# Moving small vector work to GpSimd and keeping joined weight words in PSUM, in a fused attention and two-layer MoE kernel

## The chip, the cores and the metric

The kernel runs on one core of a Trainium2 chip. The metric is the device time of one execution in microseconds (us). A core has five engines that the text names as the profile does: PE (TensorE, matrix products; PEld are its weight loads), DVE (VectorE), ACT (ScalarE), POOL (GpSimd) and SP (SyncE, which here issues nearly all DMAs). Each engine works through its own list of instructions in order and waits on semaphores for the others. PE writes its results to PSUM, a memory of eight banks of 2 KB per partition; the other data lie in SBUF. A row of scores of 768 float32 numbers takes 3 KB, and so two banks.

## What is computed

```
q_bucket, k_bucket = sign bits of q @ proj and k @ proj (6 bits), read as one number
scores = q @ k.T / 8, kept where the buckets are equal, else -1e9
attn   = softmax(scores);  x = attn @ v          # 2 batches, 8 heads, 768 x 768, head size 64
h = x @ w_in;  g = elu(h);  x2 = g @ w_out       # 1536 tokens, 512 -> 2048 -> 512
h = x2 @ w_in2;  g = s * relu(h)**2 + b;  out = g @ w_out2
```

The inputs are float64 in memory. The kernel builds float32 words from their two 32-bit halves with integer operations, and then splits each number into two float16 parts, a high one and the rest, so that three float16 products give nearly a float32 one.

## The kernel before, in words

One **unit** is one head of one block of 128 query rows: 2 x 6 x 8 = 96 units, counted u = 0 to 95 (`unit`). Of each unit, `u_s` makes the scores (four matmuls, L345), `u_soft` clamps them and takes the row's minimum on DVE (L355), makes the exponential's bias `mx` from it (L356, one number per row, DVE), and lets ACT take the exponential (L357). `u_split` transposes the result: for the first 16 units on PE (L366, L369), afterwards by splitting it into float16 parts (ACT L376, POOL L379) and a transposing DMA (L381). `u_av` multiplies by v (L393, L399). After eight units `u_norm` scales the block, casts it to float16 (L420, DVE), and takes the rest on POOL (L421).

Before the units of a batch can run, `p_split`, `p_bits` and `p_buck` prepare each pair of heads hp: they scale and split q and k (L247, L252), copy rows (L264), transpose by DMA (L270, L271, L279), copy halves of the transposed tiles (L282, L313), and add the bucket code (L307, L310, L320, L324).

Weights are made by `w_stream`, one chunk of 128 x 512 numbers at a step: a DMA loads it (L167), three DVE operations join the halves into a word (L187, L188, L190), ACT rounds it to the high part (L181), DVE takes the rest (L194). The first two joins write the PSUM tile `wx`; the third writes the SBUF tile `wa`, and both L181 and L194 read `wa`.

The order has two stages around the change. In the **first stage** the units run alone with the 16 chunks of `w_in`, until two blocks are done; PSUM then holds one score tile (`ps_s0`), two tiles for transposes and bucket codes (`ps_p0`), one bank for `wx` and one for the sums over v. In the **second stage** the products of the first layer (`moe1`: `up` gives L515 h, `down` gives L515 x2p) run, and between their steps a credit counter calls `w1_step` (16 chunks of `w_out`) and `att_step` (half a unit). PSUM then has two banks for products, two score tiles (`ps_s`, NS = 2) that also serve the bucket codes, and one bank for `wx`. Before unit 40's half step, `att_step` runs `w1_step` until all weights are made. From then on there are more buffers for the attention. The second layer (`moe2`) follows when the attention is over. A scheduler places the instructions of each engine in order of program priority and of its own estimate of when they can start; within one engine that order is then fixed.

`Ring.take(kind, ...)` gives out the pools of a kind in turn, with one counter for each kind.

Of the kernel before, what the change touches and what calls it, by code (L numbers as in the profile page):

```python
# [7 lines left out]
F32 = mybir.dt.float32  # L8
# [3 lines left out]
ACTF = mybir.ActivationFunctionType  # L12
ALU = mybir.AluOpType
PSUM = bass.MemoryType.PSUM
# [4 lines left out]
PT = 4  # L19
EX = dict(p=1, ph=1, pt=1, raw=2)  # L20
NP = 3
LOAD = [(-4, -4), (-3, -2)]
SPLIT0 = [(-4, -4), (-3, -3), (-2, -2), (0, 1)]
ENG0 = ['dve', 'act', 'act', 'act']
BITS0 = [-2, -1, 1, 3]
BUCK0 = [1, 0, 1, 1]
# [37 lines left out]
def model_kernel(tc, q, k, v, proj, w_in, w_out, w_in2, w_out2, s2, b2, sel, pop, eye, out):  # L64
# [24 lines left out]
    with ExitStack() as base:  # L89
# [18 lines left out]
        ps_w = pool(base, "ps_w", 1, space=PSUM)  # L108
        ps_s = [pool(st0, "ps_s0", S0, space=PSUM)]
        ps_p = [pool(st0, "ps_p0", P0, space=PSUM) if P0 else ps_s[0]]  # L110
        ps_m = []

        class Ring:
# [7 lines left out]
            def take(self, kind, shape, dt, name):  # L121
                pools = self.sets[kind]
                self.n[kind] += 1
                tag = "m" if kind == "w" else kind
                return pools[self.n[kind] % len(pools)].tile(shape, dt, tag=tag, name=name)
# [11 lines left out]
        ring = Ring()  # L137
        ring.use(p=[unp] * NP + [p0] * 2, ph=[un3] * NPH + [h0] * H0N, pt=[ptp] * PT + [t0_] * T0N, raw=[raw0])

        def w_raw(st):  # L140
            return pool(st, "wraw", WRAW, side="right")
# [90 lines left out]
        def p_load(b, hp, nm):  # L232
# [10 lines left out]
            raws[b, hp, nm] = t  # L243

        def scaled(eng, out, in_, sg):
            if eng == "act":
                nc.scalar.activation(out=out, in_=in_, func=ACTF.Copy, scale=sg)  # L247
            else:
                nc.vector.tensor_scalar(out, in_, sg, None, op0=ALU.mult)
# [7 lines left out]
        def p_split(b, hp, nm, eng):  # L257
# [3 lines left out]
            if nm == "k":  # L261
                hi = s_[:, :, :, 0, :]
                scaled(eng, hi, t, SQ)
                nc.vector.tensor_copy(out=s_[:, :, :, 1, :], in_=hi)  # L264
                l_ = ring.take("ph", [128, C, 2, D], F16, "srcl")
                for j in range(2):
                    rest(l_[:, :, j, :], t[:, j], SQ, hi[:, j])
                o1 = per.tile([128, 2, C, 128], F16, tag=f"k1{hp}", name=f"k1{hp}")
                o2 = per.tile([128, 2, C, 128], F16, tag=f"k2{hp}", name=f"k2{hp}")
                nc.sync.dma_start_transpose(out=full(o1), in_=s_.rearrange("p h c x d -> p (h c x d)"))  # L270
                nc.sync.dma_start_transpose(out=o2[:, 0], in_=l_.rearrange("p c x d -> p (c x d)"))  # L271
                k1[b, hp], k2[b, hp] = o1, o2
                return
# [7 lines left out]
            for j in range(2):  # L281
                nc.vector.tensor_copy(out=o2[D * j:D * j + D, j], in_=o1[D * j:D * j + D, j])  # L282
            q1[b, hp], q2[b, hp] = o1, o2
# [12 lines left out]
        def p_bits(b, hp):  # L296
            p = ps_p[0].tile([128, S], F32, tag="s", name="pbit")
            flat = lambda z: z.rearrange("p c t -> p (c t)")
# [13 lines left out]
            o = k2[b, hp]  # L312
            nc.vector.tensor_copy(out=o[D:2 * D, 1], in_=o[D:2 * D, 0])  # L313

        def p_buck(b, hp):
            t = bits.pop((b, hp))
            for x, (o, sc) in enumerate(((k2[b, hp], BK), (q2[b, hp], -BQ))):
                p = ps_p[0].tile([128, S], F32, tag="s", name="pone")
                for a0, a1 in halves:
# [19 lines left out]
        def u_s(u):  # L339
            b, c, h, hp, j = unit(u)  # L340
            p = ps_s[0].tile([128, S], F32, tag="s", name="s")
            for x, (w, m) in enumerate(((q1, k1), (q2, k2))):
# [6 lines left out]
        def u_soft(u):  # L349
# [5 lines left out]
            nc.vector.tensor_scalar(f, sps.pop(u), CLAMP, None, op0=ALU.min, op1=ALU.min, accum_out=mx)  # L355
            nc.vector.tensor_scalar(mx, mx, sm / (SQ * SQ), 10.0 * LN2, op0=ALU.mult, op1=ALU.add)  # L356
            nc.scalar.activation(out=f, in_=f, func=ACTF.Exp, scale=-sm / (SQ * SQ), bias=mx,  # L357
# [3 lines left out]
        def u_split(u, eng):  # L361
            f = pf.pop(u)
            if u < FC * H:
                p = ps_p[0].tile([128, S], F32, tag="s", name="pT")
                for cc in range(C):
# [44 lines left out]
        def u_norm(b, c):  # L410
# [8 lines left out]
            fl = xf.rearrange("p h d -> p (h d)")  # L419
            nc.vector.tensor_copy(out=xh[:, 0, :], in_=fl)  # L420
            nc.gpsimd.tensor_tensor(out=xh[:, 1, :], in0=fl, in1=xh[:, 0, :], op=ALU.subtract)  # L421
# [274 lines left out]
        if True:  # L696
# [3 lines left out]
            for hp, nm in ((0, "k"), (0, "q"), (1, "k"), (1, "q")):  # L700
# [4 lines left out]
            wst = pool(wdst, "wst", WST, side="right")  # L705
            wdec = w_raw(wdst), lambda: (wst.tile([128, 512], F32, tag="wa", name="wa"),
                                         ring.take("w", [128, 512], F32, "wx"))
            ws1 = w_stream(w_in_chunks(wi, w_in), *wdec)
# [9 lines left out]
            ring.use(m=ps_m[:])  # L718
            ps_s[0] = ps_p[0] = pool(ast, "ps_s", NS, space=PSUM)
            wop = pool(w1st, "wop", 1)  # L720
# [14 lines left out]
            def w1_step():  # L735
                if live["w1"] and next(ws1, 0) == 0:
                    live["w1"] = False
                    wdst.close()
                    ps_m.append(ps_w)
                    ring.use(m=ps_m[:])  # L740
                    ex = {k_: right(exst, f"ex_{k_}", n_) for k_, n_ in EX.items() if n_}
# [97 lines left out]
```

## Time and profile before

| | us |
|---|---|
| runs | 733.87, 735.33, 736.55 (median 735.33) |
| profiled execution | 734.32 |
| its span, first to last instruction | 732.5 |
| PE busy | 673.8 (92%) |
| DVE busy | 469.8 (64%) |
| ACT busy | 381.8 (52%) |
| POOL busy | 263.8 (36%) |

Busy time is the union of an engine's instructions. A busy PE need not be a PE at its peak, since matmuls are pipelined and their ends are modelled. The shares are means over stages with different limits, so the rows further down are taken by stage.

### The profile page before, as it was taken

How to read it: one execution, taken by the hardware profiler on the slowest of the kernel's cores; microseconds unless marked ns; L12 is line 12 of the kernel's file. 1: busy time of each engine (PE TensorE's matmuls, PEld its weight loads, DVE VectorE, ACT ScalarE, POOL GpSimd, SP SyncE). 2: the span in 40 equal slices, each digit the busy share in tenths (PEclk: the TensorE clock that was granted, in tenths of full speed). 3: DMA queues.
4: the chain of work that ended last, by engine and by line, in shares of the span. 5: the costliest groups of instructions: out<-in, count | busy, mean ns of one | idle time of the engine just before them, and what ended most of it. 6: DMA issues, size and time to landing. Idle time of an engine off the chain costs nothing.

```text
span 732.5 us, 14396 instructions
## 1 busy us (share of the span) xinstructions
PE 673.8 (92%) x5808; PEld 465.1 (63%) x5808; DVE 469.8 (64%) x874; ACT 381.8 (52%) x648; POOL 263.8 (36%) x199
## 2 busy tenths in 40 slices
PE   2779787988888999999999999999999999999998
PEld 0368666776676777888888888854444444444446
DVE  5789989989877477746744765258898989100000
ACT  2897777955698788656754413135555553010000
POOL 0000355843354388756754403124444441000000
PEclk9999979999999999999999999999999999999999
DMA  9985599999798789666658440002222214010000
GB/s 221 257 219 139 142 229 222 191 224 241 159 204 185 114 145 169 126 126 110 124 108 124 131 145 1 2 29 87 87 86 87 87 58 144 1 72 15 30 29 30
DMA packets 206594, 89.67 MB, mean 122 GB/s; under 512 B 171840, under 2 KB 203072, under 8 KB 206528
## 3 DMA queue, kind: packets, MB, share of 16 engines
q1 hardware_dynamic: 205936, 88.63, 54.8%
q8 instruction: 45, 0.74, 0.4%
q14 instruction: 21, 0.17, 0.1%
q10 hardware_dynamic: 592, 0.14, 0.1%
HBM read 43.13 MB, written 3.15 MB: 63 GB/s over the span
## 4 chain that ended last, share of the span: by engine, by line
PE 60%; DMA 13%; DVE 12%; ACT 7%; issue 6%; POOL 2%; SPq 0%; DVEq 0%; ACTq 0%; POOLq 0%
PE h L515 24%; PE y L515 17%; PE x2p L515 10%; DMA pt<-ph 8%; PE s L345 3%; PE xacc L399 3%; DVE p L355 3%; DVE e L530 2%; ACT p L357 2%; DMA q<-src 2%; POOL ph L379 1%; DVE wx L188 1%; ACT gh L535 1%; DMA k<-src 1%; ACT ph L376 1%
## 5 line engine op out<-in xcount | busy, mean ns | idle before, releaser
L379 POOL TENSOR_TENSOR ph<-p,ph 128x768 f16<-128x768 f32 x80 | 134.1, 1680 | 121.6 <-ACT ph L376 89.3
L515 PE MATMUL h<-x,wih 128*128 128x256 f16 x768 | 131.3, 275 | 0.1
L357 ACT ACTIVATE p<-p,mx 128x768 f32<-128x768 f32 x96 | 89.2, 929 | 55.1 <-DVE mx L356 53.6
L355 DVE TENSOR_SCALAR_CACHE_REDUCE p<-s 128x768 f32<-128x768 f32 x96 | 91.0, 951 | 36.9 <-PE s L345 34.5
L515 PE MATMUL x2p<-gh,wol 128*128 128x256 f16 x384 | 105.2, 275 | 1.4 <-DVE wol L194 1.4
L515 PE MATMUL x2p<-gh,woh 128*128 128x256 f16 x384 | 105.0, 275 | 1.6 <-ACT woh L181 0.9
L515 PE MATMUL x2p<-gl,woh 128*128 128x256 f16 x384 | 105.2, 275 | 0.9 <-POOL gl L538 0.8
L515 PE MATMUL h<-x,wil 128*128 128x256 f16 x384 | 105.6, 275 | 0.0
L559 POOL TENSOR_TENSOR g2l<-g,g2h 128x512 f16<-128x512 f32 x48 | 56.9, 1188 | 88.2 <-ACT g2h L556 88.2
L345 PE MATMUL s<-k,q 128*128 128x512 f16 (+1 forms) x384 | 80.8, 336 | 8.3 <-DVE p L355 7.3
L515 PE MATMUL h<-x,wi2bh 128*128 128x512 f16 x288 | 85.7, 379 | 0.0
L515 PEld LDWEIGHTS <-woh 128*128 128x128 f16 x768 | 75.2, 98 | 13.3 <-ACT woh L181 1.3
L515 PEld LDWEIGHTS <-wih 128*128 128x128 f16 x768 | 75.1, 99 | 12.4 <-issue 0.6
L538 POOL TENSOR_TENSOR gl<-g,gh 128x512 f16<-128x512 f32 x48 | 57.9, 1208 | 64.7 <-ACT gh L535 64.6
L399 PE MATMUL xacc<-vv,pt 128*128 128x64 f16 x1440 | 58.0, 196 | 19.9 <-DMA pt<-ph 19.9
L515 PE MATMUL y<-wo2l,g2h 128*128 128x512 f16 (+1 forms) x208 | 75.5, 363 | 0.0
L515 PE MATMUL y<-wo2h,g2h 128*128 128x512 f16 (+1 forms) x208 | 75.5, 363 | 0.0
L515 PE MATMUL y<-wo2h,g2l 128*128 128x512 f16 (+1 forms) x208 | 75.4, 363 | 0.0
L399 PEld LDWEIGHTS <-pt 128*128 128x128 f16 x1440 | 53.7, 100 | 28.8 <-DMA pt<-ph 25.1
L376 ACT ACTIVATE ph<-p 128x768 f16<-128x768 f32 x80 | 66.7, 836 | 5.7 <-DMA pt<-ph 4.5
L515 PEld LDWEIGHTS <-g2h 128*128 128x128 f16 x416 | 40.7, 98 | 42.5
L670 ACT ACTIVATE y<-y 128x512 f32<-128x512 f32 (+1 forms) x13 | 7.3, 564 | 97.8 <-PE y L515 96.8
(107 smaller groups left out, 1121.4 us busy)
## 6 DMA issues: line engine op xcount, KB each, us to landing
wraw<-in_moe_w_in SPq DMA_DIRECT2D x32, 512.0 KB, 3.8
wraw<-in_moe_w_out SPq DMA_DIRECT2D x32, 512.0 KB, 3.8
out<-y SPq DMA_DIRECT2D x11, 256.0 KB, 2.0
raw<-in_k SPq DMA_DIRECT2D x6, 384.0 KB, 4.4
raw<-in_q SPq DMA_DIRECT2D x6, 384.0 KB, 4.5
v<-in_v SPq DMA_DIRECT2D x4, 384.0 KB, 4.6
pt<-ph SPq DMA_TRANSPOSE x80, 4.0
x<-in_k SPq DMA_DIRECT2D x2, 384.0 KB, 5.1
```

Source lines behind the costliest of these rows:

```text
L188: nc.vector.scalar_tensor_tensor(out=x, in0=low, scalar=29, in1=x, op0=ALU.logical_shift_right, op1=ALU.bitwise_or)
L345: nc.tensor.matmul(p[:, a0:a1], w[b, hp][:, j, c, :], kf[:, a0:a1], start=(x == 0), stop=(x == 1))
L355: nc.vector.tensor_scalar(f, sps.pop(u), CLAMP, None, op0=ALU.min, op1=ALU.min, accum_out=mx)
L357: nc.scalar.activation(out=f, in_=f, func=ACTF.Exp, scale=-sm / (SQ * SQ), bias=mx, accum_out=sums[b, c][:, h:h + 1])
L376: nc.scalar.activation(out=t[:, 0, :], in_=f, func=ACTF.Copy)
L379: nc.gpsimd.tensor_tensor(out=t[:, 1, :], in0=f, in1=t[:, 0, :], op=ALU.subtract)
L399: nc.tensor.matmul(acc, o[:, C * x + cc, :], vv[:, j, cc, y, :], start=(z == 0 and cc == 0), stop=(z == 2 and cc == C - 1))
L515: nc.tensor.matmul(p, ws[a](kk), xs[b](kk), start=(kk == 0 and z == 0), stop=(kk == n_kk - 1 and z == 2))
L530: nc.vector.tensor_scalar(t["e"], t["e"], SG, -SG, op0=ALU.mult, op1=ALU.add)
L535: nc.scalar.activation(out=gh, in_=t["g"], func=ACTF.Copy)
L538: nc.gpsimd.tensor_tensor(out=gl, in0=t["g"], in1=gh, op=ALU.subtract)
L559: nc.gpsimd.tensor_tensor(out=gl, in0=t["g"], in1=gh, op=ALU.subtract)
```

## The change

- The bias `mx` of units 0 to 43 (`MXP = 44`) is computed on POOL instead of DVE.
- For head pairs 2 and 3 of the first batch, the row copies L264, L282 and L313 go to POOL (`side`): 2 + 4 + 2 instructions.
- The cast L420 goes to ACT for blocks 2 to 5 of the first batch.
- In the second stage the joined word of a `w_out` chunk stays in the PSUM tile: L190 writes `wx` in place, and L181 and L194 read it there. The word tiles rotate over three banks: the one of before and two new ones (`ps_w2`).
- The two banks come from the scores: from the start of the second stage until the weights are made there is one score tile (`lent`), which the bucket codes share; afterwards the second comes back (`ps_s2`).
- Score tiles and bucket-code tiles are now taken through `Ring` as two kinds, "s" and "s2", each with its own counter.

```diff
+MXP = 44
...
-        ps_s = [pool(st0, "ps_s0", S0, space=PSUM)]
-        ps_p = [pool(st0, "ps_p0", P0, space=PSUM) if P0 else ps_s[0]]
+        ps_s = pool(st0, "ps_s0", S0, space=PSUM)
+        ps_p = pool(st0, "ps_p0", P0, space=PSUM)
...
-                tag = "m" if kind == "w" else kind
+                tag = {"w": "m", "s2": "s"}.get(kind, kind)
...
+                 s=[ps_s], s2=[ps_p])
...
+        def side(b, hp):
+            return nc.gpsimd if b == 0 and hp > 1 else nc.vector
...
-                nc.vector.tensor_copy(out=s_[:, :, :, 1, :], in_=hi)
+                side(b, hp).tensor_copy(out=s_[:, :, :, 1, :], in_=hi)
...
-                nc.vector.tensor_copy(out=o2[D * j:D * j + D, j], in_=o1[D * j:D * j + D, j])
+                side(b, hp).tensor_copy(out=o2[D * j:D * j + D, j], in_=o1[D * j:D * j + D, j])
...
-            p = ps_p[0].tile([128, S], F32, tag="s", name="pbit")
+            p = ring.take("s2", [128, S], F32, "pbit")
...
-            nc.vector.tensor_copy(out=o[D:2 * D, 1], in_=o[D:2 * D, 0])
+            side(b, hp).tensor_copy(out=o[D:2 * D, 1], in_=o[D:2 * D, 0])
...
-            p = ps_s[0].tile([128, S], F32, tag="s", name="s")
+            p = ring.take("s", [128, S], F32, "s")
...
-            nc.vector.tensor_scalar(mx, mx, sm / (SQ * SQ), 10.0 * LN2, op0=ALU.mult, op1=ALU.add)
+            (nc.gpsimd if u < MXP else nc.vector).tensor_scalar(mx, mx, sm / (SQ * SQ), 10.0 * LN2, op0=ALU.mult, op1=ALU.add)
...
-            nc.vector.tensor_copy(out=xh[:, 0, :], in_=fl)
+            if FC <= b * C + c < C:
+                nc.scalar.activation(out=xh[:, 0, :], in_=fl, func=ACTF.Copy)
+            else:
+                nc.vector.tensor_copy(out=xh[:, 0, :], in_=fl)
...
-            wdec = w_raw(wdst), lambda: (wst.tile([128, 512], F32, tag="wa", name="wa"),
-                                         ring.take("w", [128, 512], F32, "wx"))
+
+            def words():
+                x = ring.take("w", [128, 512], F32, "wx")
+                return (x if len(more) else wst.tile([128, 512], F32, tag="wa", name="wa")), x
+
+            more = []
+            wdec = w_raw(wdst), words
...
-            ps_s[0] = ps_p[0] = pool(ast, "ps_s", NS, space=PSUM)
+
+            lent = pool(ast, "ps_s", 1, space=PSUM)
+            ring.use(s=[lent], s2=[lent])
+            more.append(pool(wdst, "ps_w2", 2, space=PSUM))
+            ring.use(w=[ps_w] + more * 2)
...
                     ps_m.append(ps_w)
+                    own = [lent, pool(ast, "ps_s2", 1, space=PSUM)]
+                    ring.use(s=own, s2=own)
```

## Rows read from the trace of the kernel before

**Rows 1.** Windows by stage: stretch, its length, busy us (count) by engine, clock, DMA share, GB/s.
```profile
29.00:92.50 63.50, 53.74 (x434) 42.29 (x433) 59.66 (x130) 51.44 (x85) 7.92 (x5) 0.99 0.67 183
92.50:172.40 79.90, 69.11 (x795) 55.03 (x795) 74.89 (x145) 58.71 (x105) 48.60 (x31) 0.92 1.06 215
172.40:186.00 13.60, 11.22 (x133) 9.15 (x134) 12.47 (x20) 5.59 (x10) 1.64 (x1) 1.00 0.82 210
186.00:312.00 126.00, 112.69 (x1346) 90.53 (x1344) 91.32 (x174) 99.24 (x167) 75.91 (x52) 0.99 0.87 161
312.00:732.50 420.50, 416.78 (x3049) 264.38 (x3046) 214.62 (x365) 154.49 (x266) 129.08 (x100) 1.00 0.30 74
```

**Rows 2.** The chain that ended last, shares by line, in 29:92.5, 92.5:172.4 and 172.4:186.
```profile
by line: DVE p L355 20.1%; DMA q<-src 13.2%; issue 9.1%; DVE wx L188 9.0%; DVE wil L194 8.3%; PE xacc L393 8.2%; DVE wx L187 6.8%; PE pT L366 4.5%; PE s L345 4.1%; DVE wa L190 3.1%; ACT p L357 3.1%; DVE vv L291 1.6%; DVE bits L310 1.5%; ACT
...
by line: DMA pt<-ph 36.2%; issue 18.3%; PE h L515 14.6%; POOL ph L379 6.4%; PE xacc L399 4.5%; ACT p L357 3.1%; DVE p L355 2.6%; DVE wx L188 2.5%; PE s L345 2.5%; DVE wx L187 2.4%; ACT ph L376 2.0%; DVE wa L190 0.8%; DVE g L532 0.8%; ACT e 
...
by line: DVE wol L194 22.7%; PE h L515 20.4%; DVE wa L190 15.4%; DVE wx L188 13.6%; DVE wx L187 10.2%; PE x2p L515 6.3%; ACT ph L376 6.2%; ACT woh L181 3.9%; issue 1.7%
```

**Rows 3.** DVE and ACT groups in 92.5:186: shapes, count, busy us, mean ns, idle before.
```profile
L194 DVE SCALAR_TENSOR_TENSOR wol<-wa,woh 128x512 f16<-128x512 f32 x16 | 18.2, 1139 | 1.3 <-ACT woh L181 1.1
...
L420 DVE CAST xh<-xf 128x512 f16<-128x512 f32 x2 | 0.8, 416 | 0.0
...
L535 ACT ACTIVATE gh<-g 128x512 f16<-128x512 f32 x8 | 5.0, 619 | 0.5 <-DVE g L532 0.5
```

**Rows 4.** Lines L194, L616, L532, whole span: ns min/median/max, first and last start.
```profile
L194 DVE SCALAR_TENSOR_TENSOR wol<-wa,woh x16: 677/1112/1868, 115.6 to 183.1; 128x512 f16<-128x512 f32 x16
...
L616 DVE SCALAR_TENSOR_TENSOR x<-x2p,x x12: 679/691/693, 156.8 to 481.4; 128x512 f16<-128x512 f32 x12
...
L532 DVE SCALAR_TENSOR_TENSOR g<-h,e x48: 676/691/693, 104.8 to 463.0; 128x512 f32<-128x512 f32 x48
```

**Rows 5.** DVE in order of time, two of the L194: start, us, instruction.
```profile
134.93 1.60 DVE L194 SCALAR_TENSOR_TENSOR wol<-wa,woh 128x512 f16<-128x512 f32 x1
...
173.82 1.77 DVE L194 SCALAR_TENSOR_TENSOR wol<-wa,woh 128x512 f16<-128x512 f32 x1
```

**Rows 6.** Order of time, copies of head pair 3, a transpose; in brackets idle before.
```profile
23.83 0.36 DVE L264 COPY src<-src 128x768 f16<-128x768 f16 x1 [2.29 <-ACT src L247]
...
26.08 2.41 SPq L270 DMA_TRANSPOSE k<-src  x1
...
33.78 0.36 DVE L313 COPY k<-k 64x768 f16<-64x768 f16 x1
...
41.34 0.72 DVE L282 COPY q<-q 64x768 f16<-64x768 f16 x2 [1.83 <-DMA q<-src]
```

**Rows 7.** POOL groups, whole span, columns as in rows 3.
```profile
L379 POOL TENSOR_TENSOR ph<-p,ph 128x768 f16<-128x768 f32 x80 | 134.1, 1680 | 121.6 <-ACT ph L376 89.3 <-issue 24.9 <-POOL gl L538 3.0
...
L822 POOL MEMSET const-float32-1.0<- 128x1 f32 x1 | 0.1, 98 | 0.0
```

**Rows 8.** DVE in order of time: the bias L356 and what stands around it.
```profile
44.30 0.15 DVE L356 TENSOR_SCALAR mx<-mx 128x1 f32<-128x1 f32 x1
44.37 0.68 DVE L194 SCALAR_TENSOR_TENSOR wil<-wa,wih 128x512 f16<-128x512 f32 x1
...
122.66 0.94 DVE L355 TENSOR_SCALAR_CACHE_REDUCE p<-s 128x768 f32<-128x768 f32 x1
...
126.33 0.14 DVE L356 TENSOR_SCALAR mx<-mx 128x1 f32<-128x1 f32 x1
```

**Rows 9.** PE's waits in 29:93 (first) and 93:175: total us, times, longest.
```profile
PE s L345 <- DVE p L355: 5.1, 5, 1.5
...
PE xacc L399 <- DMA pt<-ph: 9.8, 9, 2.9
...
PE s L345 <- DVE p L355: 0.9, 1, 0.9
```

**Rows 10.** PE in order of time: a score tile made ahead of its reader.
```profile
118.72 0.81 PE L345 MATMUL s<-k,q 128*128 128x512 f16 x4
```

More of the change, by code (lines that the diff above doesn't have):

```diff
@@ L137, in model_kernel @@
         ring = Ring()
-        ring.use(p=[unp] * NP + [p0] * 2, ph=[un3] * NPH + [h0] * H0N, pt=[ptp] * PT + [t0_] * T0N, raw=[raw0])
+        ring.use(p=[unp] * NP + [p0] * 2, ph=[un3] * NPH + [h0] * H0N, pt=[ptp] * PT + [t0_] * T0N, raw=[raw0],
+                 s=[ps_s], s2=[ps_p])
         def w_raw(st):
@@ L317, in p_buck @@
             for x, (o, sc) in enumerate(((k2[b, hp], BK), (q2[b, hp], -BQ))):
-                p = ps_p[0].tile([128, S], F32, tag="s", name="pone")
+                p = ring.take("s2", [128, S], F32, "pone")
                 for a0, a1 in halves:
@@ L363, in u_split @@
             if u < FC * H:
-                p = ps_p[0].tile([128, S], F32, tag="s", name="pT")
+                p = ring.take("s2", [128, S], F32, "pT")
                 for cc in range(C):
```

## The prediction

> **What bounds the kernel now.** I read the busy time by stage first, because the page's shares mix stages with different limits [rows 1]. Behind 312 us PE is busy 416.8 of 420.5 us; no part of the change touches that stretch, and it can only move as a whole. Between 186 and 312 PE idles 13.3 us, and there only the two counters and two casts change. What the change aims at lies before 186. In 29 to 92.5 us, the units of the first stage, DVE is busy 59.7 of 63.5 us. In 92.5 to 172.4, the second stage, DVE is busy 74.9 of 79.9 us and PE 69.1. In 172.4 to 186, where the last weights are forced out before unit 40, DVE has 12.5 of 13.6 us and PE 11.2. So DVE is the fullest engine all the way, but PE is not far below it: it has 9.8, 10.8 and 2.4 us to give.
>
> A full engine need not be the one that the end waits for, so the second view is the chain of waits for the same three stretches [rows 2]. In the first it runs mostly over DVE (L355 20%, the word operations behind it), with 13% in one transpose `q<-src`. In the second the longest part is the attention's transpose `pt<-ph`, 36%; the DVE lines shown are 2.6% and less, and part of DVE's work hides in "issue", 18%. In the third four DVE word operations make 62%. A microsecond saved on DVE should therefore be worth nearly a microsecond in the first and third stretch, and clearly less in the second.
>
> **The joined words.** In the second stage L194 takes 1.139 us in the mean, 18.2 us for 16 [rows 3]. Its shortest is 0.677 and its longest 1.868 us, though all have one shape. L616 and L532 are the same operation on as many numbers, except that their first input lies in PSUM; 60 of them lie between 0.676 and 0.693 us, between 104.8 and 481.4 us, with POOL about as busy for most of it [rows 1, 4]. So it is the two SBUF inputs that make L194 meet POOL, and with the word in PSUM I expect 0.69. That frees 18.2 - 16 x 0.69 = 7.2 us of DVE. Of this, the excess in places where the chain runs on DVE is certain to count: five L194, from 134.93 to 173.82 (1.60, 0.91, 1.60, 1.05 and 1.77 us), 6.93 - 5 x 0.69 = 3.5 us (the first and the last of them stand in [rows 5]). The others shorten a queue in front of L355 and with it the way to the next `pt`. Between 3.5 and 7.2 I take -5.0, nearer the lower end since `pt<-ph` leads the chain there; the lower bound of the gain is 0, if that transpose hides it all. That L190 writes PSUM instead of SBUF I cost at nothing: in the third stretch's chain L188, which writes PSUM already, has 13.6% and L190 15.4%, so the write to PSUM is not the dearer one [rows 2]. L181 from PSUM is at the worst unchanged, since ACT idles 21 of 80 us [rows 1].
>
> [...]
>
> **The copies.** Of the eight copies five lie before 29 us, where DVE waits anyway: L264 of pair 3 comes after 2.29 us of idling, ends at 24.19 and is first needed by the transpose issued at 26.08. Of the others, L313 takes 0.36 us and the two L282 0.72, and in front of L282 DVE stood 1.83 us for a transpose with its whole queue behind it [rows 6]. All of it off DVE is 2.9 us, on the first stage's DVE chain. On POOL a copy costs something between DVE's 0.36 us and the 1.68 us that POOL's two-input L379 takes on 128 x 768 [rows 7]; I take 0.9, nearer the middle. The dearest one, 1.3 us late, still fits the 1.9 us before the transpose, and POOL is otherwise free there (7.9 of 63.5 us). But the same wait now stops POOL's queue: behind L282 stand the biases of the next units, and ACT's exponentials wait for them. No DMA is moved, and POOL issues none here; SP's transposes only wait for another engine's copy. So I take -2.0; bounds -2.9 and 0.
>
> **The biases.** L356 lasts 0.15 us but the next instruction starts 0.07 us later [rows 8]. Of the 44, some 42 lie before 186 us: 42 x 0.07 = 2.9 us of DVE. A third of the first chain is not DVE's, and most of the second is not, so -1.0; bounds -2.9 and 0. On POOL one costs between the 0.10 us of a 128 x 1 MEMSET and 1.68 [rows 7]; with so few numbers I take 0.2. In the first stage POOL is nearly empty. In the second it is busy 48.6 of 79.9 us, so a bias waits behind half of an L379 six times in ten, about 0.5 us in the mean. Now it waits on DVE: after the L355 of 122.66 it came at 126.33, 2.7 us behind that one's end [rows 8]. I take the delay as even, 0, with +2.5 as a bound, for ten biases a quarter of a microsecond worse.
>
> **The cast** leaves DVE with 0.42 us and takes ACT 0.62 [rows 3], twice before 186 us and twice behind. ACT has the room; -0.3, bounds -0.8 and 0.
>
> **One score tile instead of two.** From 92.5 us until the weights are done about 20 units must wait with their scores until L355 has read the unit before. Now PE works ahead: the scores of 118.72 were made while the tile before them was read only at 122.66 [rows 8, 10]. Behind a waiting score matmul stand the products of the first layer on PE. The nearest row is the first stage, which has one score tile already: 5.1 us in five waits over 20 units, against 0.9 in the second with two [rows 9]. There PE had little else to do; here the scheduler has products to place in between, and a faster DVE reads sooner. I take +1.5, with 0 and +5 as bounds.
>
> **The counters.** Behind 186 us "s" and "s2" count separately over two tiles, where they took turns before. Some of the 12 bucket-code tiles will now fall on the tile just filled. If every third waits one L355 of 0.95 us, that is +4; PE has other work, so I take +0.5; bounds 0 and +4.
>
> **The sum.** -5.0 - 2.0 - 1.0 - 0.3 + 1.5 + 0.5 = -6.3 us on the profiled execution's 734.3 us (its span 732.5 and 1.8 around it), which gives 728.0. The median of the runs is 1.0 us above that execution, so against it I forecast 729.0. What can be told from no change is about 0.3%, 2.2 us.
>
> **Rivals.** *DVE pays in full* (0.20). If "issue" and `pt<-ph` in the second stretch are only echoes of a late DVE, the terms go to their far ends, -7.2 - 2.9 - 2.9 - 0.3, with +1.5 for the scores: -11.8, 723.5. For it speaks DVE's 94% there; against it that PE has 13 us to give in both stretches and can't use all of it.
>
> *The transpose hides it* (0.14). The attention in the second stage goes at the pace of `pt<-ph`, for which PE waits 9.8 us [rows 9], and a faster DVE merely waits longer. Then of the words only the L194 of 173.82 counts, 1.1 us, with -2.0 from the copies and +2.0 of costs: 734.
>
> *Slower through the lent score tile* (0.12). PE's list is fixed, and a score matmul that comes up before L355 has read its tile holds all products behind it. In the row above that is from 119.4 to 123.6, 4 us. If eight units used the second tile and lose 2 us each, +16 against -8.3 makes 743. It decides from 1 us for each of the eight.
>
> *POOL gets in the way* (0.10). Copies and biases read SBUF on POOL, and DVE's two-input operations beside them stretch as L194 did, by up to 1.2 us [rows 4]; the copies then give back what they saved, and the biases queue behind L379: 728.0 + 2.0 + 2.5 + 1.0 = 733.5 against the runs. For it speaks that DVE is full there, so some operation always stands beside a copy; against it, that three copies are few.
> [...]
>
> **How the numbers follow.** The forecast has 0.44, the rivals 0.20, 0.14, 0.12 and 0.10. The forecast and the full payment are faster by over 0.3%, and of the rest about half of the POOL case: 0.69. Within 0.3% end the hidden case and the other half less a little: 0.16. Slower are the lent tile and some of the counters' bound: 0.15. The range starts at 720: the bounds of all gains without a cost, -13.8, are 721.5, and POOL's L379, which meet fewer L194, get the rest. It ends at 737, above the two cases near the old time; it leaves out the lent tile's case and little else. The likeliest case by itself is 725 to 732.
>
> **What would show it.** Right: L194 `wol` at 0.69 us without long ones; no DVE wait in front of an L282 at 40 us; the last L194 `wol`, which starts at 183.1 us now [rows 4], 5 to 8 us sooner. Wrong: L194 still above 1 us; PE waiting for L355 by more than 5 us in the second stage; biases on POOL more than 2.7 us behind their L355 [rows 8]; a later end of the attention although the weights are done sooner.

## The result, and the profile after

The changed kernel is slower: 739.0 us median (738.0 to 743.0, six runs) beside 734.75 us of the kernel before on the same chip, a ratio of 1.0077 with a 95% interval of 1.0055 to 1.0098. The forecast was 729.0, with a range up to 737. The medians alone differ by 4.3 us, the ratio by 5.6; below, the ratios are used. The profiled execution spans 737.8 us (before 732.5). Its mean granted clock is 0.972 (before 0.988), but that is not the loss: another execution of the changed kernel with 0.988 took 738.1 us.

The windows of the changed kernel over the stretches of [rows 1]:

```profile
29.00:92.50 63.50, 54.25 (x412) 41.70 (x409) 59.12 (x105) 49.65 (x85) 10.79 (x23) 0.93 0.64 184
92.50:172.40 79.90, 67.76 (x743) 54.62 (x744) 67.50 (x124) 55.85 (x99) 46.28 (x47) 0.90 0.96 208
172.40:186.00 13.60, 12.61 (x160) 10.28 (x159) 5.82 (x12) 8.38 (x15) 7.50 (x9) 1.00 0.86 147
186.00:312.00 126.00, 111.04 (x1312) 88.46 (x1310) 79.86 (x163) 94.43 (x161) 72.30 (x52) 0.97 0.88 154
312.00:737.80 425.80, 421.71 (x3136) 268.06 (x3132) 217.65 (x376) 162.13 (x279) 135.69 (x105) 1.00 0.33 78
```

The third busy time of a row is DVE's. DVE did become free: it is busy 67.5 us instead of 74.9 in the second stage, 5.8 instead of 12.5 in the third stretch. PE got nothing from it: 743 matmuls (x) in the second stage instead of 795, 1312 instead of 1346 from 186 to 312, and 87 more are left for the end (3136 against 3049), 4.9 us of PE.

The words, by their line (L194 before, L196 now), as [rows 4]; and POOL's groups from 0 to 186 us:

```profile
L196 DVE SCALAR_TENSOR_TENSOR wol<-wx,woh x16: 637/681/691, 103.1 to 167.4; 128x512 f16<-128x512 f32 x16
...
L361 POOL TENSOR_SCALAR mx<-mx 128x1 f32<-128x1 f32 x41 | 9.6, 235 | 57.2 <-DVE p L360 53.2 <-DVE rs L418 2.7
...
L287 POOL COPY q<-q 64x768 f16<-64x768 f16 x4 | 3.3, 823 | 5.3 <-DMA q<-src 5.2
...
L269 POOL COPY src<-src 128x768 f16<-128x768 f16 x2 | 2.4, 1213 | 20.8 <-ACT src L252 20.8
```

No long L196 is left, and the last one starts at 167.4 us instead of 183.1. Waits of the changed kernel, ACT's from 29 to 186 us, PE's from 92.5 to 175 and DVE's from 92.5 to 186 (us, times, longest), with DVE's of the kernel before as the last line:

```profile
ACT p L362 <- POOL mx L361: 23.7, 17, 3.7
...
PE s L350 <- DVE p L360: 0.4, 1, 0.4
...
DVE p L360 <- PE s L350: 12.5, 8, 3.0
DVE wx L189 <- DMA wraw<-in_moe_w_out: 7.5, 6, 1.9
...
DVE p L355 <- PE s L345: 2.3, 3, 1.6
```

PE does not stand for the one score tile. DVE does: it waits 12.5 us for scores, and 7.5 us for raw weights, for which it did not wait before. ACT's long wait is not the bias's own delay: from the start of L360 to the exponential pass 2.0 us in the mean of units 4 to 40, no more than before (2.5 in units 4 to 19, 3.4 in 20 to 40). What is late is the attention itself. I count its units by L360 (L355 before), from 0. Unit 38, the first `k<-src` of the second batch on SP's queue and the first bucket bits of the second batch, in the kernel before, in order of time:

```profile
164.07 0.94 DVE L355 TENSOR_SCALAR_CACHE_REDUCE p<-s 128x768 f32<-128x768 f32 x1
...
186.05 1.45 SPq L270 DMA_TRANSPOSE k<-src  x1
...
202.44 0.95 DVE L310 TENSOR_SCALAR bits<-pbit 128x768 f16<-128x768 f32 x1
```

and in the changed kernel:

```profile
173.29 13.27 SPq L386 DMA_TRANSPOSE pt<-ph  x5
...
179.68 0.96 DVE L360 TENSOR_SCALAR_CACHE_REDUCE p<-s 128x768 f32<-128x768 f32 x1 [2.40 <-PE s L350]
...
186.67 1.96 SPq L275 DMA_TRANSPOSE k<-src  x1
...
211.44 0.96 DVE L315 TENSOR_SCALAR bits<-pbit 128x768 f16<-128x768 f32 x1 [2.30 <-DMA k<-src]
```

Unit 38 is 15.6 us late although the weights are ready 15.7 us sooner. The weights then wait for the attention. SP issues five transposes of the late units, one after another as they become ready, until 186.6 us, so the second batch's `k<-src` behind them starts no sooner than before, and the first bits come 9 us later.

A ledger says where this becomes time. I value each matmul by its columns, 0.109 us for 256. That is the median from one start to the next where products of 256 columns follow each other in the kernel before; 512 columns take 0.216 us there and 64 columns 0.029, so the value is an estimate from the trace. The f32 matmuls of the first chunks are put at four times that per column: those of 64 columns take 0.112 us, near their value, those of 128 columns 0.109, half of it. They are the same in all kernels, so this shifts all sums alike. I add the values up to a moment and subtract the sum from the moment: what PE has lost till then. A matmul that lies across 186 or 240 us counts on both sides, which makes the last two losses up to 0.7 us too small. In all kernels below but one the span less the loss at 312 us lies between 680.1 and 683.6 us, so the loss at 312 us decides. Lost by 92.5, 186, 240 and 312 us: before 20.1, 41.8, 47.8, 51.8; changed 21.2, 42.8, 54.2, 55.9. Of the 4.1 us at 312 only 1.0 stands at 186; the rest comes behind it, while the second batch is prepared.

### The profile page after: what moved, and what is told of

It reads as the page before. It is cut to its first block, busy times and chain, and to the rows that moved or that the text cites. A ratio compares the mean times of both kernels' runs of the same rounds, so it can differ in the third digit from the quotient of the medians.

```text
span 737.8 us, 14396 instructions
## 1 busy us (share of the span) xinstructions
PE 677.6 (92%) x5808; PEld 467.1 (63%) x5808; DVE 446.1 (60%) x818; ACT 383.3 (52%) x652; POOL 278.9 (38%) x251
## 3 DMA queue, kind: packets, MB, share of 16 engines
q1 hardware_dynamic: 205936, 88.63, 55.1%
## 4 chain that ended last, share of the span: by engine, by line
PE 53%; DVE 4%; ACT 3%; DMA 2%; issue 2%; POOL 1%; DVEq 0%; ACTq 0%; POOLq 0%
PE h L523 22%; PE y L523 17%; PE x2p L523 9%; PE xacc L404 3%; PE s L350 3%; DVE e L538 1%; DMA pt<-ph 1%; DVE g L540 1%; ACT gh L543 1%; ACT e L531 1%; ACT p L362 1%; DMA wraw<-in_moe_w_in 1%; ACT ph L381 1%; DVE p L360 0%; DMA x<-xh 0%
## 5 line engine op out<-in xcount | busy, mean ns | idle before, releaser
L384 POOL TENSOR_TENSOR ph<-p,ph 128x768 f16<-128x768 f32 x80 | 132.0, 1656 | 94.9 <-ACT ph L381 52.7
L360 DVE TENSOR_SCALAR_CACHE_REDUCE p<-s 128x768 f32<-128x768 f32 x96 | 90.8, 950 | 44.2 <-PE s L350 41.7
L350 PE MATMUL s<-k,q 128*128 128x512 f16 (+1 forms) x384 | 82.4, 340 | 8.5 <-DVE p L360 7.2
L523 PEld LDWEIGHTS <-wih 128*128 128x128 f16 x768 | 74.9, 99 | 16.7 <-issue 5.2
```

Of the source, the lines that this page charges most:

```text
L350: nc.tensor.matmul(p[:, a0:a1], w[b, hp][:, j, c, :], kf[:, a0:a1], start=(x == 0), stop=(x == 1))
L384: nc.gpsimd.tensor_tensor(out=t[:, 1, :], in0=f, in1=t[:, 0, :], op=ALU.subtract)
L523: nc.tensor.matmul(p, ws[a](kk), xs[b](kk), start=(kk == 0 and z == 0), stop=(kk == n_kk - 1 and z == 2))
```

## The experiments

The theory was first that the lent tile makes the attention late; rivals were the biases and the copies on POOL. All ratios are to the kernel before, with 95% intervals; 0.1% is 0.73 us.

**Parts taken back.** Biases on DVE again:

```diff
-MXP = 44
+MXP = 0
```

> The changed kernel, with every bias back on DVE; the joined words, the lent score tile and the copies on POOL stay as changed. Theory 'lent tile' (with one score tile instead of two the attention of the second stage runs 12 to 16 us late, and that is what costs): unit 38 still starts L360 at 176 us or later (before 164.1, changed 179.7), and the time stays within 2 us of the changed kernel, 737 to 741. Rival 'biases' (ACT waits 26 us for mx, which stands on POOL behind L384, the residual of xh and the q copies): the exponentials come 2 to 3 us behind L360 again without the longer ones, unit 38 starts by 172 us, and the time falls to 732 to 736, all or most of the loss of 4.3 us.

1.0091 (1.0061 to 1.0120), unit 38 at 181.6 us: no better, the biases are not the loss.

Copies on DVE again:

```diff
-            return nc.gpsimd if b == 0 and hp > 1 else nc.vector
+            return nc.vector
```

> The changed kernel, with the eight copies of pairs 2 and 3 back on DVE; biases on POOL and joined words as changed. Theory 'lent tile': 737 to 741, and unit 38 still at 176 us or later. Rival 'copies' (POOL waits 5.2 us at 33 us for the transpose of q with two biases behind it, so units 2 and 3 reach their exponentials 2.7 and 4.7 us later than before): units 2 and 3 come back to about 34.5 and 41 us, unit 15 starts 2 us sooner (77.5), and 1 to 2 us of that reach the end, 736 to 738.

1.0009 (0.9986 to 1.0033). Unit 3 starts at 34.8 us instead of 38.0, unit 15 at 76.8 instead of 79.6, and some 5 us come back; yet unit 38 is as late as ever, 183.2. So the copies cost here, in another place than the theory's.

Words in SBUF and two score tiles again:

```diff
-            lent = pool(ast, "ps_s", 1, space=PSUM)
-            ring.use(s=[lent], s2=[lent])
-            more.append(pool(wdst, "ps_w2", 2, space=PSUM))
-            ring.use(w=[ps_w] + more * 2)
+            both = pool(ast, "ps_s", NS, space=PSUM)
+            ring.use(s=[both], s2=[both])
...
-                    own = [lent, pool(ast, "ps_s2", 1, space=PSUM)]
-                    ring.use(s=own, s2=own)
...
-                return (x if len(more) else wst.tile([128, 512], F32, tag="wa", name="wa")), x
+                return wst.tile([128, 512], F32, tag="wa", name="wa"), x
```

> The changed kernel, with words joined in SBUF as before and two score tiles, with one rotation for scores and preparation, from the second stage on; biases, copies and the two casts stay moved. Theory 'lent tile': unit 38 starts by 166 us, the last words stay near 183 us, and the time falls below before's 734.8 by the 1 to 3 us that DVE saves in the first stage: 731.5 to 734. Rival 'POOL' (biases and copies on POOL cost it): slower than before still, 737 to 740, and unit 38 late at 172 us or more though two score tiles stand there.

0.9968 (0.9947 to 0.9988), unit 38 at 161.7 us: faster than before, with everything but the words and the tile. Its `wol` row, columns as above:

```profile
L196 DVE SCALAR_TENSOR_TENSOR wol<-wa,woh x16: 676/1208/2028, 108.9 to 182.2; 128x512 f16<-128x512 f32 x16
```

The words alone (the three edits of bias_dve, copies_dve and the casts undone together):

```diff
-            if FC <= b * C + c < C:
-                nc.scalar.activation(out=xh[:, 0, :], in_=fl, func=ACTF.Copy)
-            else:
-                nc.vector.tensor_copy(out=xh[:, 0, :], in_=fl)
+            nc.vector.tensor_copy(out=xh[:, 0, :], in_=fl)
```

> The kernel before with one part of the change: words joined in PSUM in banks lent by the second score tile, and the two counters after the weights; biases, copies and casts are on DVE as before. Theory 'lent tile': the loss is all here, 737 to 741, unit 38 at 176 us or later, the last words at 167 to 170 us. Rival 'POOL': the words pay, unit 38 by 168 us, and the time is 729 to 732, some 5 us less than before.

1.0032 (1.0011 to 1.0052), unit 38 at 181.0 us, last `wol` at 170.0. By itself this part loses 2.4 us. The next four take it apart; each is an edit of words_only.

**Tile, counter, bank.** One score tile, words in SBUF (with the last edit of words_old):

```diff
-            more.append(pool(wdst, "ps_w2", 2, space=PSUM))
-            ring.use(w=[ps_w] + more * 2)
```

> The kernel before with one score tile in the second stage, until the weights are made, and the two counters after it; words are joined in SBUF as before, and the two lent banks stand empty. Theory 'lent tile': the missing tile alone makes the attention late, so unit 38 starts at 176 us or later and the time is that of the joined words with the lent tile (737.2) or the up to 3 us more that the words save there: 736 to 741. Rival 'order of the words' (words that come at another pace from PSUM push the attention back): unit 38 within 4 us of before's 164.1, and 734 to 736.

1.0034 (1.0019 to 1.0048), last `wol` at 181.7 us. The time is that of words_only, but unit 38 starts at 171.2 us: the missing tile accounts for 7 of the 17 us, and the words in PSUM push the attention back by another 10. The theory explains only a part.

Two score tiles, words joined in place in one bank (shown in part; the lines on `own` go as in words_old, and `w_stream` gets `inplace` as an argument):

```diff
-            lent = pool(ast, "ps_s", 1, space=PSUM)
-            ring.use(s=[lent], s2=[lent])
-            more.append(pool(wdst, "ps_w2", 2, space=PSUM))
-            ring.use(w=[ps_w] + more * 2)
+            both = pool(ast, "ps_s", NS, space=PSUM)
+            ring.use(s=[both], s2=[both])
+            more.append(ps_w)
...
+                    early = done and inplace and len(more)
+                    if early:
+                        nc.vector.scalar_tensor_tensor(out=lo, in0=w, scalar=SW, in1=hi,
+                                                       op0=ALU.mult, op1=ALU.subtract)
```

> The kernel before with words joined in place in the one bank they had, from the second stage on, so that the rest (L196) reads PSUM; it is issued ahead of the next chunk's join. Two score tiles stand throughout, with one rotation; biases, copies and casts are on DVE. Theory 'lent tile': the shorter L196 pays what it can where no tile is lent, unit 38 stays at 165 us or sooner, and the time is 730 to 734. Rival 'the words were never worth anything' (the transposes of the attention lead that stretch): 734 to 736. A third: with one bank DVE waits for ACT's cast between chunks, and the time is above 736.

1.0201 (1.0177 to 1.0225), the third case. Waits of DVE and of ACT from 110 to 200 us, and the line of the words:

```profile
DVE wol L188 <- ACT woh L185: 11.9, 12, 2.7
...
ACT woh L185 <- DVE wx L198: 20.4, 7, 2.9
...
L188 DVE SCALAR_TENSOR_TENSOR wol<-wx,woh x16: 674/690/692, 114.5 to 197.4; 128x512 f16<-128x512 f32 x16
```

With one bank DVE and ACT take turns, the last `wol` is 14.3 us later than before, and the kernel 2.0%, 14.8 us, slower, though unit 38 starts at 157.3. Here the late weights cost about their whole delay, and the early attention brought nothing back.

One counter for both tiles after the weights:

```diff
                 pools = self.sets[kind]
+                kind = "s" if kind == "s2" and pools is self.sets["s"] else kind
```

> The words in PSUM with the lent tile alone (737.2), but one counter for scores and preparation once the second tile is back, so the two always alternate. Theory 'lent tile': the loss is made before, unit 41 starts near 187 us as without, and the time is 736 to 738.5. Rival 'two counters' (a preparation tile stands on the scores' tile while the other is free): units 44 to 52 come 5 us or more sooner than with two counters (206.0 and 258.6), and the time falls to 733 to 735.5.

1.0044 (1.0023 to 1.0065), unit 52 at 261.0 us: the counters are not it.

Two banks for words instead of three:

```diff
-            more.append(pool(wdst, "ps_w2", 2, space=PSUM))
-            ring.use(w=[ps_w] + more * 2)
+            more.append(pool(wdst, "ps_w2", 1, space=PSUM))
+            ring.use(w=[ps_w] + more)
```

> The lent tile with joined words alone (737.2), with two banks for words instead of three (the fourth stands empty). Theory 'words crowd in' (with three banks more chunks are under way, their word operations go ahead of L360 on DVE, and the attention falls a further 10 us back beside what the missing tile costs): unit 38 starts at 170 to 174 us as with one tile and words in SBUF (171.2, with three banks 181.0), the last words come at 174 to 180 us instead of 170, and the time stays at 735 to 737.5, since the end needs both. Rival 'tile alone': unit 38 stays at 178 us or later.

0.9902 (0.9878 to 0.9926), 727.2 us. Unit 38 and the last `wol` came where the theory had them, 171.2 and 177.3 us, but the time fell far below what it said: one bank fewer turns a loss into the largest gain of all. DVE in words_only, from one L360 to the next, in order of time:

```profile
122.11 0.95 DVE L360 TENSOR_SCALAR_CACHE_REDUCE p<-s 128x768 f32<-128x768 f32 x1
...
123.58 0.68 DVE L190 SCALAR_TENSOR_TENSOR wx<-wraw,wx 128x512 int32<-128x512 int32 x1
124.18 0.68 DVE L196 SCALAR_TENSOR_TENSOR wol<-wx,woh 128x512 f16<-128x512 f32 x1
...
125.44 0.68 DVE L196 SCALAR_TENSOR_TENSOR wol<-wx,woh 128x512 f16<-128x512 f32 x1
126.03 0.68 DVE L192 SCALAR_TENSOR_TENSOR wx<-wraw,wx 128x512 int32<-128x512 int32 x1
126.63 0.69 DVE L189 TENSOR_SCALAR wx<-wraw 128x512 int32<-128x512 int32 x1
...
128.18 0.68 DVE L189 TENSOR_SCALAR wx<-wraw 128x512 int32<-128x512 int32 x1
...
129.37 0.69 DVE L190 SCALAR_TENSOR_TENSOR wx<-wraw,wx 128x512 int32<-128x512 int32 x1
129.96 0.68 DVE L196 SCALAR_TENSOR_TENSOR wol<-wx,woh 128x512 f16<-128x512 f32 x1
130.56 0.95 DVE L360 TENSOR_SCALAR_CACHE_REDUCE p<-s 128x768 f32<-128x768 f32 x1
```

In the 8.4 us between these two L360 DVE does eight word operations, and nowhere stands still: with three banks up to three chunks can be under way, and their operations stand ahead of the next unit. In DVE's order 29 of the 32 chunks are finished before unit 33 in words_only and in the changed kernel, 25 in two_banks and one_tile, 22 in the kernel before. The rows of the two kernels that show what comes of it: the chain from 92.5 to 172.4 us by line, DVE's wait for raw weights from 92.5 to 186, SP's queue, and the windows; first words_only:

```profile
by line: DMA wraw<-in_moe_w_out 28.2%; issue 11.2%; DMA x<-xh 7.4%; DVE wx L192 7.0%; DVE wx L190 6.7%; DVE p L360 6.7%; DMA pt<-ph 6.7%; PE h L520 6.1%; DVE wx L189 5.8%; DVE wol L196 5.4%; DVE g L537 3.9%; DVE xh L425 1.6%; PE xacc L404 1
...
DVE wx L189 <- DMA wraw<-in_moe_w_out: 7.0, 8, 2.3
...
172.85 15.44 SPq L386 DMA_TRANSPOSE pt<-ph  x5
188.39 1.76 SPq L275 DMA_TRANSPOSE k<-src  x1
...
172.40:186.00 13.60, 12.83 (x150) 10.75 (x149) 6.00 (x16) 9.03 (x16) 7.33 (x6) 1.00 0.90 147
...
240.00:312.00 72.00, 66.21 (x817) 53.44 (x817) 47.74 (x103) 54.66 (x92) 47.53 (x33) 0.98 0.80 135
```

and two_banks:

```profile
by line: DMA pt<-ph 37.3%; DMA wraw<-in_moe_w_out 12.6%; issue 10.4%; DVE wx L190 6.3%; DVE p L360 4.3%; PE xacc L404 3.9%; PE h L520 3.7%; ACT p L362 2.9%; DVE wil L196 2.6%; DVE wx L189 2.5%; PE s L350 2.5%; DVE wx L192 2.3%; ACT ph L381 
...
DVE wx L189 <- DMA wraw<-in_moe_w_out: 3.9, 2, 2.1
...
180.40 2.12 SPq L275 DMA_TRANSPOSE k<-src  x1
...
172.40:186.00 13.60, 13.60 (x162) 10.93 (x159) 9.32 (x26) 10.73 (x20) 6.56 (x4) 1.00 0.86 169
...
240.00:312.00 72.00, 70.90 (x894) 58.40 (x892) 46.15 (x106) 55.04 (x95) 52.54 (x35) 0.99 0.85 141
```

With three banks the words run ahead until DVE stands waiting for their data, and the chain is theirs. With two the attention's transposes lead the chain again, `k<-src` goes out 8 us sooner, PE is never idle from 172.4 to 186 us, and from 240 to 312 it has 4.7 us more work. That the gain of 9.6 us between the two comes by this way is likely, not shown: cast_2b below has unit 38, the last `wol` and `k<-src` each 2 to 3 us sooner still, and is slower than two_banks.

**The parts on POOL and ACT**, each against the kernel before (words and tiles as in words_old). First biases and casts, without the copies, from words_old:

```diff
-            return nc.gpsimd if b == 0 and hp > 1 else nc.vector
+            return nc.vector
```

> The kernel before with the biases of 44 units on POOL and two casts on ACT, and nothing else: words in SBUF, two score tiles, copies on DVE. Theory 'copies' (on POOL they cost 3.9 us in the changed kernel, which had 739.0 with and 735.1 without): here too they stand ahead of the biases, so without them units 3 and 15 start 3 us sooner than with them (38.4, 79.9), and the time is 728 to 730. Rival: with two score tiles the copies' delay is made up again before the end, and the time is that with copies, 730 to 732.

0.9927 (0.9908 to 0.9946), 728.25 us. Against words_old the copies make 3 us, and units 3 and 15 start 3.6 and 3.0 us sooner. Then the biases alone, from that, with DVE's cast again:

```diff
-            if FC <= b * C + c < C:
-                nc.scalar.activation(out=xh[:, 0, :], in_=fl, func=ACTF.Copy)
-            else:
-                nc.vector.tensor_copy(out=xh[:, 0, :], in_=fl)
+            nc.vector.tensor_copy(out=xh[:, 0, :], in_=fl)
```

> The kernel before with the biases of units 0 to 43 on POOL and nothing else. Theory 'late biases' (on DVE a bias of 0.15 us stands behind whatever is queued after L360, so the exponential comes 2 to 5 us behind L360; on POOL 1.3 to 2 us): the exponentials come sooner, unit 38 starts by 159 us, and nearly all of the gain of biases and casts together is here, 728 to 730. Rival 'casts' (the two casts of 1.03 us off DVE carry a good part): 731 to 733.

0.9973 (0.9957 to 0.9990). The exponential follows its L360 by 2.0 us in the mean of units 4 to 19 (before 2.5) and 2.5 in units 20 to 40 (3.4). A real gain, but less than a half of that with casts. The casts alone, from bias_cast:

```diff
-MXP = 44
+MXP = 0
```

> The kernel before with the casts of chunks 2 to 5 on ACT and nothing else. Biases alone gave -1.6 us and biases with casts -5.2. Theory 'casts pay' (1.03 us on DVE stands before L360 and the words at 110 to 190 us): 729 to 731.5. Rival 'only together' (the sum is one of the order in which the program's scheduler puts the rest): 732.5 to 735.

1.0004 (0.9986 to 1.0021). So -5.3 us for both is not the sum of -2.0 and +0.3: either the two help each other, or the order that the program's scheduler writes happened to be a good one. No run tells which. The copies alone, from words_old, with DVE's biases and casts (the edits of cast_only and bias_only):

> The kernel before with the eight copies of pairs 2 and 3 on POOL and nothing else: no bias stands behind them there. Theory 'head of the queue' (they cost because the biases on POOL wait behind them): 732.5 to 735.5, no loss, and the DVE time freed in the first stage may show. Rival 'slow copy' (1.20 us against 0.36 us puts the preparation of pairs 2 and 3 itself late): unit 15 starts 1 us or more behind before's 77.4, and the time is 735.5 to 738.

0.9992 (0.9972 to 1.0011), unit 15 at 78.7 us: the slow copy shows there and is made up again. The copies alone cost nothing.

All 96 biases on POOL, from bias_cast:

```diff
-MXP = 44
+MXP = 96
```

> Biases and two casts moved, copies on DVE, two score tiles (728.25), with the biases of all 96 units on POOL. Theory 'late biases': behind unit 44 the products of TensorE fill the time, so the rest gives little, 726.5 to 728.5. Rival 'POOL fills' (L384 of 1.7 us stands ahead of the later biases, with POOL busy 65 to 73% from 186 to 312 us): 729 to 732, and ACT waits over 10 us for mx between 186 and 312 us.

1.0067 (1.0041 to 1.0093). Up to 312 us it has lost 49.1 us, less than before; it alone of all kernels loses behind that. From 186 to 312 us ACT's wait for `mx` is 12.6 us on POOL against 11.7 on DVE in bias_cast, but from 312 to 420 it is 31.3 against 26.6, and PE stands 5.0 us there for the attention (2.8 for `xf`, 2.2 for `pt`), where in bias_cast it does not wait. So the late biases on POOL cost, later than the rival had them and more: the kernel ends some 8 us above the rival's range.

**Does it hold in the changed kernel?** The changed kernel with the edit of two_banks:

```diff
-            more.append(pool(wdst, "ps_w2", 2, space=PSUM))
-            ring.use(w=[ps_w] + more * 2)
+            more.append(pool(wdst, "ps_w2", 1, space=PSUM))
+            ring.use(w=[ps_w] + more)
```

> The changed kernel with two banks for words instead of three (the fourth stands empty); biases, copies and casts stay moved. Theory 'words crowd in' (the third bank lets word operations go ahead of L360, and that made the loss): as in the kernel with the words alone (737.2 with three, 727.2 with two), the time falls well below the changed kernel's 739.0, to 730 to 735, and unit 38 starts by 176 us (179.7). Rival 'chance of the order' (the ten us are this one order's luck): 737 to 741 as before.

1.0014 (0.9986 to 1.0041) instead of 1.0077: 4.6 us back, at the slow end of the theory's range. Its sign did not come: unit 38 starts at 177.8 us, 1.9 sooner than with three banks and not by 176. In DVE's order 27 chunks instead of 29 stand before unit 33; in the words alone it was 25. Three banks with two raw tiles, from words_only:

```diff
-WRAW = 3
+WRAW = 2
```

> Words in three PSUM banks with the lent tile alone (737.2), but two tiles for the raw weights instead of three, so that fewer chunks are under way. In DVE's order 28 instead of 32 of the 32 chunks then stand ahead of unit 38, as 30 with two banks. Theory 'words crowd in': the number under way decides and not the bank, so unit 38 starts at 168 to 174 us and the time is 726 to 732. Rival 'third bank' (something of the bank itself): 736 to 739. A third: with two raw tiles the transfers come later, and the last words at 185 us or later, 733 to 738.

0.9985 (0.9968 to 1.0002), unit 38 at 170.6 us as with two banks. For the attention it is enough to limit the chunks under way; the third bank itself does no harm. But the last `wol` now comes at 182.8 us, and most of two_banks' gain is missing.

after_2b with the copies on DVE:

```diff
-            return nc.gpsimd if b == 0 and hp > 1 else nc.vector
+            return nc.vector
```

> The same with the copies of pairs 2 and 3 back on DVE: words in two PSUM banks with the lent tile, 44 biases on POOL, two casts on ACT. If the gains of two banks (6.2 us) and of biases with casts (5.2 us) add up: 721 to 724, faster than any so far. Rival 'one bound' (both pay by the same words and attention before 186 us, so only the larger counts): 726 to 730.

1.0064 (1.0042 to 1.0085). Neither theory; here taking the copies back loses 3.7 us, where it won 5 in the changed kernel. `k<-src` goes out at 183.1 us, so it is not the mechanism above; by the ledger it has lost less than before at 240 us (46.3) and more at 312 (55.1).

best_2b is also copies_dve with two banks instead of three, and read so it goes against the theory: unit 38 comes 7.7 us sooner and `k<-src` 7.5 us sooner, and the kernel is 0.55% slower, 4.0 us. It differs from two_banks, too, only by the biases on POOL and the casts on ACT, which gave -5.3 us in bias_cast; beside two banks they cost 11.8. No trace here shows why.

Unit 38 does not tell the time, then. The first bits of the second batch do so better. Of the ten kernels that have them by 203.0 us, nine span 725.9 to 733.4 us (the tenth is bias_all, which loses behind 312); of the ten that have them at 207.8 or later, among them best_2b with 208.4, all span 732.9 or more. That the two go together does not show a cause.

**How much is the order's?** The changed kernel with four biases back on DVE:

```diff
-MXP = 44
+MXP = 40
```

> The changed kernel with the biases of units 40 to 43 on DVE, those of 0 to 39 on POOL: four operations of 0.15 us differ, and with them the order that the program's scheduler writes behind unit 40. If the loss of the changed kernel has its cause before unit 40 (three banks, the copies), the time stays within 1.5 us of 739.0. If a good part is the luck of one order, it moves by 2 us or more, to either side, and single differences of 2 to 3 us between the kernels here mean nothing by themselves.

1.0120 (1.0083 to 1.0157). Up to unit 42 every L360 I compared stands within 1.1 us of the changed kernel's, and from unit 50 to 70 within 0.4; the loss is there in both, and 0.4% more here, with intervals that overlap. The six executions lie between 739.0 and 748.7 us, and the profiled one is the second fastest, so its trace can't show what the others lose. two_banks with the casts of chunks 2 to 5 on ACT:

```diff
-            nc.vector.tensor_copy(out=xh[:, 0, :], in_=fl)
+            if FC <= b * C + c < C:
+                nc.scalar.activation(out=xh[:, 0, :], in_=fl, func=ACTF.Copy)
+            else:
+                nc.vector.tensor_copy(out=xh[:, 0, :], in_=fl)
```

> Words in two PSUM banks with the lent tile (727.2 alone), with two casts of xh on ACT; biases and copies on DVE. The same number of chunks stands ahead of each unit on DVE as without the casts. Theory 'two banks pay where the attention is not put behind': 725.5 to 729. If the gain was the luck of one order: 731 or more.

0.9962 (0.9944 to 0.9979): the gain survives, less by 4.4 us. Edits that should change little but the order move the time by 3 to 4 us, and the biases and casts of best_2b by more, so single differences of that size prove nothing here. More chunks under way was slower in three kernel pairs (words_only to two_banks 1.3%, words_only to raw2 0.5%, changed to after_2b 0.6%) and faster in the fourth (copies_dve to best_2b, 0.55%). That the third bank puts the attention back is shown; what that costs in time is not the same from kernel to kernel.

## Why the prediction was wrong

**The words, -5.0: the step that failed.** Its first half was right: L196 at 0.68 us, none long, 0.46 us less each; the last words were forecast 5 to 8 us sooner and came 15.7 sooner. Wrong was "the others shorten a queue in front of L355 and with it the way to the next `pt`". The change also gave the words a third bank, and I priced what that does to DVE's order at nothing. Further word operations went ahead of L360, until DVE stood waiting, 7.5 us for raw weights and 12.5 for scores: the freed time did not reach the next `pt`. Measured over one_tile, which has the same tile and counters, the words give -0.1 us with three banks and -9.7 with two (1.0032 and 0.9902 against 1.0034). With two raw tiles (raw2) they give -3.6. So a gain was there to be had where fewer chunks are under way; its size rests on single orders and stays open. I had also looked for the effect before 186 us; by the ledger 3.1 of the 4.1 us come behind it, where I expected only the counters and two casts.

**One score tile and the counters, +2.0.** Together +2.5 us (1.4 to 3.5) in one_tile: about right, by another way than I said. PE hardly waits (0.4 us, forecast by the first stage's 5.1 us [rows 9]); the attention falls 7 us back. The rival "slower through the lent score tile" ended on the right side with 743, by the wrong mechanism: it decided from 1 us of PE's waiting for each of eight units, and there was 0.4 in all.

**Biases, casts, copies, -3.3.** Together -0.32%, -2.3 us (-3.9 to -0.9) in words_old: near as a sum, and that is partly luck. Apart they measure -2.0, +0.3 and -0.6 us, biases with casts -5.3, of which the copies then take 3.0 back. A bias mostly costs 0.19 us on POOL (taken 0.2); the eight copies 0.82 to 1.47 us, 1.05 in the mean (taken 0.9). The queue that I named is there: POOL stands 5.17 us for `q<-src`, and a bias behind it, in the changed kernel:

```profile
38.45 1.71 POOL L287 COPY q<-q 64x768 f16<-64x768 f16 x2 [5.17 <-DMA q<-src]
40.24 0.19 POOL L361 TENSOR_SCALAR mx<-mx 128x1 f32<-128x1 f32 x1
```

The ground of "POOL gets in the way" holds: in the kernel before, all eleven L194 `wol` over 0.75 us run while POOL is busy, and the four beside which it stands still take 0.69 (one of 0.68 us runs beside POOL too). By what the two meet, no trace shows. That the moved work made it worse isn't shown. POOL is busy 58.0 us of the second stage in words_old and 58.8 in bias_only (before 48.6), and the median L196 in SBUF is 1.208 us in the one and 0.692 in the other (before 1.112 [rows 4]). A first input in PSUM costs L196 nothing that shows: its median in the changed kernel is 681 ns from PSUM, and the shortest L194 from SBUF in the kernel before takes 677.

**What stays open.** The parts measured alone sum to +2.4 - 2.3, about zero; the changed kernel has +5.6 us by its ratio. So the words' term explains 4.9 of the 11.9 us between forecast (-6.3) and result, and some 5.5 us belong to no part by itself. In the changed kernel 4.6 us go with the third bank (after_2b), and 5.0 with the copies (copies_dve), but with both taken back (best_2b) the loss is there again. Why the copies cost 5 us beside three banks and gain 3.7 beside two, the runs don't settle; the cause of that part stays open. The sign named in the prediction, "a later end of the attention although the weights are done sooner", came true.

## What to carry to other kernels

Here the time freed on DVE went to what stood next in its order, eight word operations in the 8.4 us between two L360 of words_only. So ask which of two streams will take freed time, and which of them the end is waiting for; here the weights came 15.7 us sooner and then waited for an attention that was 15.6 us late. The number of banks set how far the words ran ahead, 29 of the 32 chunks before unit 33 in words_only with three and 25 in two_banks: try one buffer fewer. Here that gave 1.3% in one kernel, 0.6% in another, and lost 0.55% in a third. So where a scheduler writes the order, repeat an edit in a second kernel before the difference is believed, and count every pair, those that disagree too.

## What I had not expected of the hardware

POOL's copy of 128 x 768 f16 takes 1.21 us in the changed kernel where DVE's takes 0.36 [rows 6], and of 64 x 768, half the partitions, it takes 0.82 to 1.47 us. The cast of xh on DVE, 0.42 us undisturbed [rows 3], took 1.03 us at 127.22 us in words_only, and up to 1.87 elsewhere there.
